# Two experts with an early part of 256 slots, and a denser routing of the last chunk but one

## The chip, the cores and the metric

The kernel runs as one program on one core of a Trainium2 chip. The metric is the device time of an execution in microseconds (us): the median of three runs.

## The reference, cut to what matters

Three layers follow one another. The first is an attention (2 batches, 8 heads, 768 positions, head size 64) in which a query sees only the keys of its own hash bucket. The second is a dense layer of 512 to 2048 to 512. The third, which the change is about, sends each of 1536 tokens to two of eight experts:

```python
noisy_logits = x @ w_gate + np.log1p(np.exp(x @ w_noise)) * noise
top2 = np.argpartition(-noisy_logits, 2, axis=1)[:, :2]
top2_l = np.take_along_axis(noisy_logits, top2, axis=1)
top2_w = np.exp(top2_l - top2_l.max(-1, keepdims=True))
top2_w /= top2_w.sum(-1, keepdims=True) + 1e-09
for e in range(8):
    for k in range(2):
        mask = top2[:, k] == e
        h = np.maximum(x[mask] @ w1[e], 0.0)          # 512 -> 1024
        out[mask] += top2_w[mask, k, None] * (h @ w2[e])   # 1024 -> 512
```

## The kernel before, in words

**Chunks.** Tokens go through attention and the dense layer in six chunks of 256 (ci 0 to 5). The order of the work is a loop over steps g: the attention has NU = 96 steps, and the loop runs 20 steps beyond. In each step a chunk of the dense layer has one of its sixteen pieces (i): eight of `h` (L460, 24 matmuls of 256 columns) and eight of `px` (L471, 12 matmuls of 512 columns), so a step of the tail is about 2.6 us of TensorE. Chunk 5 has the steps 99 to 114.

**Order.** Functions are put on lists for a step: `start` (ahead of the step's work), `soon` (after its activations), `at` (at its end). From step 100 on, the instructions of every engine, SyncE's DMA queue among them, stand in the order in which these lists emit them (`tc.manual_schedule`). Within one list the plain functions go first to last, and generators (the routing) then take turns.

**Routing.** `route(ci)` (L572) computes the gate with sixteen small matmuls into `pz`, and then some forty tiny VectorE operations with ScalarE exponentials between them; `yield 1` marks where the chain goes from one engine to the other (a hop). Its end are slot numbers `si` (L679) and four indirect DMAs of GpSimd (the scatters, L685) that write each token's row of values and metadata into `slots` in DRAM. Each expert has 400 slots (CAP). Chunk 4's routing begins in step 103 and takes a hop a step; its last part is emitted in step 110. Chunk 5's routing is spread over the first steps of the experts, eight small operations a step from step x = 2.

**Experts.** In the second loop, over x, each expert's slots are read by a transposing DMA into `xg` (`e_load`, L749, with the metadata `mt` behind it on SyncE's queue), `e_meta` (L768) makes weights and token numbers of the metadata in small VectorE operations, `l1` (L799) and `l1_out` (ScalarE L809, VectorE L810) make the hidden layer through three PSUM buffers `ph`, and `l2` (L821; its last, half-filled tile L825) and `l2_out` (ScalarE L835, then an adding scatter of GpSimd L838) the output. Weights are loaded in eight blocks of 512 KB an expert (`w12_load`, L724, SyncE's queue, four buffers `w`), and each block is split into two fp16 halves by ScalarE (L742) and VectorE (L743) in `w12_split`. Expert 0's blocks 4 to 7 are loaded in steps 107 to 110 and its splits are in steps 107 to 114. The buffers of expert 1's weights are those of the dense layer's `wo`.

**The early part.** Of the first EA = 1 experts, the first 256 slots are a part of their own. After chunk 4, `reserve` raises the count of such an expert to 256 at least, so that chunk 5's tokens go behind these slots, and this part can run while chunk 5 is still being routed. The order of parts is (0,0), (0,1), (1,0), (2,0), ...; a name (e,p) is expert e, part p.

Of the kernel before, what the change touches and what calls it, by code (L numbers as in the profile page):

```python
# [52 lines left out]
SW2 = 2.0 ** 6  # L53


PARAM = dict(GM=16, HE=lambda nm, b: 'D', OE=lambda nm, b: 'D', SC=lambda nm, b: 'D', WB=0, XO=lambda b: 'D', NG=16, WS=lambda i: 'P', TS=lambda g: True, XL=lambda g: 'D', GW=2, E0=7, T0=12, T1=16, EL=8, WX=3, PV={(1,2,3):4}, PVD=5, ST={}, VA={}, RA={}, O0=48, OS=2, IS=2, FU=16, VF=2, EC=lambda g: 'AA', QX=8, QS=3, EA=1, S1=(8,8,8,9,9,9,11,13), QE=8, XG=2, XB=2, PC=2, OH=3, BK=3, R0=18, R1=0, LK=8, WL=1, NW=3, LE=lambda nc: nc.scalar, I0=24, LQ=8, LV=0, W=[(g, 1) for g in range(-6, 30)], KA={(0,0,0):-8,(0,0,1):-6,(0,1,0):-4,(0,1,1):-2}, QA={(0,0,0):-7,(0,0,1):-3}, HI=lambda g: 'P', LO=lambda g: False)
PARAM.update(KA={(0, 0, 0): -15, (0, 0, 1): -6, (0, 1, 0): -5, (0, 1, 1): -4, (0, 2, 0): -1, (0, 2, 1): 1, (0, 3, 0): 4, (0, 3, 1): 5, (1, 0, 0): 37, (1, 0, 1): 39, (1, 1, 0): 44, (1, 1, 1): 46, (1, 2, 0): 42, (1, 2, 1): 51, (1, 3, 0): 47, (1, 3, 1): 51}, QA={(0, 0, 0): -15, (0, 0, 1): -3, (0, 0, 2): 1, (0, 0, 3): 3, (0, 1, 0): 8, (0, 1, 1): 9, (0, 1, 2): 17, (0, 1, 3): 21, (0, 2, 0): 24, (0, 2, 1): 28, (0, 2, 2): 30, (0, 2, 3): 33, (1, 0, 0): 37, (1, 0, 1): 41, (1, 0, 2): 47, (1, 0, 3): 52, (1, 1, 0): 57, (1, 1, 1): 56, (1, 1, 2): 60, (1, 1, 3): 69, (1, 2, 0): 72, (1, 2, 1): 69, (1, 2, 2): 80, (1, 2, 3): 84}, VA={(0, 0, 0): -1, (0, 0, 1): -3, (0, 1, 0): -1, (0, 1, 1): -1, (0, 2, 0): 0, (0, 2, 1): 0, (0, 3, 0): -1, (0, 3, 1): -2, (1, 0, 0): -1, (1, 0, 1): -1, (1, 1, 0): 2, (1, 1, 1): -4, (1, 2, 0): -3, (1, 2, 1): -3, (1, 3, 0): 2, (1, 3, 1): -2}, PV={(0, 0, 0): 4, (0, 0, 1): 5, (0, 0, 2): 6, (0, 0, 3): 5, (0, 1, 0): 6, (0, 1, 1): 4, (0, 1, 2): 4, (0, 1, 3): 5, (0, 2, 0): 5, (0, 2, 1): 5, (0, 2, 2): 5, (0, 2, 3): 6, (1, 0, 0): 4, (1, 0, 1): 5, (1, 0, 2): 4, (1, 0, 3): 5, (1, 1, 0): 5, (1, 1, 1): 5, (1, 1, 2): 5, (1, 1, 3): 6, (1, 2, 0): 6, (1, 2, 1): 4, (1, 2, 2): 4, (1, 2, 3): 4}, RA={0: 18, 1: 18, 2: 19, 3: 24, 4: 18}, W=[(g,1) for g in [-6, -4, -3, -1, 0, 0, 1, 1, 2, 4, 4, 7, 8, 8, 9, 10, 11, 12, 13, 14, 15, 16, 16, 17, 18, 20, 20, 22, 22, 23, 23, 24]], EC=lambda g:'AA', LE=lambda nc:nc.sync, HI=lambda g:'AAAA'[g%4], LO=lambda g:[0, 0, 0, 1, 0, 0, 0, 1][g%8]==1, S1=[8, 8, 8, 8, 8, 11, 13, 22], ST={0: 4, 1: 4, 2: 5, 3: 4, 4: 5, 5: 3}, NG=28, WS=lambda i:'PAAA'[i%4], HE=lambda nm,b:'DPDD'[2*(nm=='k')+b], OE=lambda nm,b:'DTDD'[2*(nm=='k')+b], SC=lambda nm,b:'DADD'[2*(nm=='k')+b], R1=2, I0=26, IS=1, O0=56, OS=1, GM=100, BK=3, OH=3, QX=8, QS=2, QE=7, VF=0, T0=12, T1=17, EL=10, WX=5, WL=2, PC=2, GW=2, E0=8, WB=2)


@with_exitstack  # L60
def fused(ctx: ExitStack, tc: tile.TileContext, q, k, v, proj, w_in, w_out, w_gate, w_noise, noise,
          w1, w2, out, dbg=None):
    nc = tc.nc
# [784 lines left out]
    def at(g, f, *a):  # L848
        todo.setdefault(g, []).append((f, a))

    def start(g, f, *a):
# [4 lines left out]

    def piece(gen):
        for x in gen:
            if x:
                return  # L860
            yield
# [98 lines left out]
    for g in range(g_lo, G1 + 1):  # L960
# [7 lines left out]
        prev = steps.get(g - 1, [])  # L968
# [183 lines left out]
```

## Time and profile before

| | us |
|---|---|
| median of 3 runs (lowest, highest) | 825.37 (823.86, 825.7) |
| the profiled execution | 823.72 |
| its span | 822.0 |
| TensorE busy | 715.9 (87%) |
| VectorE busy | 533.9 (65%) |
| ScalarE busy | 445.0 (54%) |
| GpSimd busy | 267.9 (33%) |

The span runs from the first to the last instruction; what lies around it is 1.72 us. Busy time is a mean over stages with different limits. The change is about the hand-over from the dense layer to the experts, at 500 to 610 us of the span, so that stretch is read by itself: for each engine its instructions in order of time, with the idle time before one and what ended it.

### The profile page before, as it was taken

How to read it: one execution, taken by the hardware profiler on the slowest of the kernel's cores; microseconds unless marked ns; L12 is line 12 of the kernel's file. 1: busy time of each engine (PE TensorE's matmuls, PEld its weight loads, DVE VectorE, ACT ScalarE, POOL GpSimd, SP SyncE). 2: the span in 40 equal slices, each digit the busy share in tenths (PEclk: the TensorE clock that was granted, in tenths of full speed). 3: DMA queues.
4: the chain of work that ended last, by engine and by line, in shares of the span. 5: the costliest groups of instructions: out<-in, count | busy, mean ns of one | idle time of the engine just before them, and what ended most of it. 6: DMA issues, size and time to landing. Idle time of an engine off the chain costs nothing.

```text
span 822.0 us, 14816 instructions
## 1 busy us (share of the span) xinstructions
PE 715.9 (87%) x5398; PEld 446.0 (54%) x5399; DVE 533.9 (65%) x1330; ACT 445.0 (54%) x859; POOL 267.9 (33%) x303
## 2 busy tenths in 40 slices
PE   1676478988988888898999999879999999999995
PEld 1343345646754665466568576547554655556553
DVE  8998799997896789569869526454633525345210
ACT  3778767766765686467567425234533534334220
POOL 6444646560444055314212132241021120311212
PEclk9878789999999999999999999999999999999998
DMA  8999689999999999995797542856875858677213
GB/s 218 224 251 212 180 187 184 255 277 218 175 171 195 154 200 192 225 159 106 119 176 123 102 156 88 221 146 180 250 158 173 199 111 232 135 194 176 28 19 47
DMA packets 268126, 140.04 MB, mean 170 GB/s; under 512 B 224720, under 2 KB 243856, under 8 KB 268048
## 3 DMA queue, kind: packets, MB, share of 16 engines
q1 hardware_dynamic: 261520, 125.37, 68.1%
q0 software_dynamic: 6528, 13.68, 9.3%
q8 instruction: 43, 0.70, 0.4%
q14 instruction: 35, 0.29, 0.1%
HBM read 61.48 MB, written 23.79 MB: 104 GB/s over the span
## 4 chain that ended last, share of the span: by engine, by line
PE 42%; DVE 5%; DMA 3%; POOL 2%; issue 1%; ACT 1%; POOLq 0%; ACTq 0%; DVEq 0%
PE ph L799 15%; PE py L821 13%; PE px L471 6%; PE h L460 3%; PE py L825 2%; DVE er L323 1%; DMA xg<-slots 1%; PE pv L368 1%; POOL slots L685 1%; DMA slots<-xr,si 1%; DMA et<-er 1%; PE s L254 1%; ACT er L314 1%; DVE e L266 1%; DVE th L490 1%
## 5 line engine op out<-in xcount | busy, mean ns | idle before, releaser
L460 PE MATMUL h<-xt,wi 128*128 128x256 f16 x1152 | 140.2, 277 | 6.2 <-DVE mx L279 3.2
L799 PE MATMUL ph<-xg,ew 128*128 128x400 f16 (+2 forms) x864 | 135.4, 320 | 8.9 <-DMA xg<-slots 8.4
L743 DVE SCALAR_TENSOR_TENSOR ew<-w,ew 128x1024 f16<-128x1024 f32 x64 | 77.9, 1226 | 88.2 <-ACT ew L742 88.0
L471 PE MATMUL px<-wo,gt 128*128 128x512 f16 x576 | 132.6, 382 | 0.5 <-DVE th L490 0.4
L460 PEld LDWEIGHTS <-wi 128*128 128x128 f16 x1152 | 112.5, 99 | 28.2 <-issue 9.1
L821 PE MATMUL py<-ew,ht 128*128 128x512 f16 x576 | 125.8, 379 | 0.0
L838 POOL DMA_INDIRECT out_dram<-yo,ti x32 | 51.2, 1600 | 216.7 <-ACT yo L835 216.7
L254 PE MATMUL s<-kt,qt 128*128 128x512 f16 (+1 forms) x384 | 88.2, 353 | 33.3 <-DVE mx L266 28.5
L799 PEld LDWEIGHTS <-ew 128*128 128x128 f16 x864 | 82.6, 100 | 59.8 <-issue 6.8
L275 ACT ACTIVATE e<-e,mx 128x768 f32<-128x768 f32 x96 | 89.4, 931 | 27.9 <-DVE mx L266 21.5
L505 POOL TENSOR_TENSOR gt<-th,gt 128x512 f16<-128x512 f32 x48 | 60.1, 1252 | 122.0 <-ACT gt L504 121.6
L266 DVE CUSTOM_DVE_ANT_0 e<-s,zero 128x768 f32<-128x768 f32 x96 | 90.6, 948 | 4.4 <-PE s L254 1.5
L821 PEld LDWEIGHTS <-ht 128*128 128x128 f16 x576 | 56.3, 98 | 67.0
L471 PEld LDWEIGHTS <-gt 128*128 128x128 f16 x576 | 55.3, 98 | 64.1 <-issue 3.2
L323 DVE SCALAR_TENSOR_TENSOR er<-e,mx,er 128x768 f16<-128x768 f32 x68 | 73.1, 1080 | 25.9 <-ACT er L314 25.3
L314 ACT ACTIVATE er<-e,mx 128x768 f16<-128x768 f32 x68 | 63.0, 930 | 37.8 <-DMA et<-er 21.6
L835 ACT ACTIVATE yo<-py,wv 128x512 f32<-128x512 f32 (+1 forms) x32 | 20.3, 633 | 102.4 <-PE py L821 54.6
L809 ACT ACTIVATE ht<-ph 128x400 f16<-128x400 f32 (+2 forms) x72 | 33.5, 466 | 73.0 <-PE ph L799 72.9
L254 PEld LDWEIGHTS <-qt 128*128 128x128 f16 x384 | 37.0, 103 | 62.7 <-issue 38.5
L810 DVE SCALAR_TENSOR_TENSOR ht<-ph,ht 128x400 f16<-128x400 f32 (+2 forms) x72 | 37.6, 524 | 49.5 <-ACT ht L809 49.5
L742 ACT ACTIVATE ew<-w 128x1024 f16<-128x1024 f32 x64 | 66.3, 1047 | 2.6 <-DMA w<-in_moe_w_dram 2.6
L368 PE MATMUL pv<-et,vt 128*64 128x256 f16 x720 | 51.2, 284 | 7.5 <-DMA et<-er 7.5
(195 smaller groups left out, 945.8 us busy)
## 6 DMA issues: line engine op xcount, KB each, us to landing
w<-in_moe_w_dram SPq DMA_DIRECT2D x64, 512.0 KB, 4.6
wraw<-in_moe_w_in_dram SPq DMA_DIRECT2D x16, 512.0 KB, 4.6
wraw<-in_moe_w_out_dram SPq DMA_DIRECT2D x16, 512.0 KB, 4.3
slots<-blank SPq DMA_DIRECT2D x6, 1032.0 KB, 6.8
v<-in_v_dram SPq DMA_DIRECT2D x24, 192.0 KB, 4.1
out_dram<-zeros SPq DMA_DIRECT2D x13, 256.0 KB, 3.4
k<-in_k_dram SPq DMA_DIRECT2D x16, 192.0 KB, 3.6
q<-in_q_dram SPq DMA_DIRECT2D x24, 128.0 KB, 3.1
```

The costliest lines, as they stand in the source:

```text
L254: nc.tensor.matmul(ps[:, n0 * 128:n1 * 128], qt[:, s, h, t, :], kt[:, s, h, n0:n1, :].rearrange("p c t -> p (c t)"), start=(s == 0), stop= ...
L266: nc.vector.tensor_tensor_reduce(e32, st[g]["ps"][:, :S], zero.to_broadcast([128, S]), -0.125, TOP, op0=OP.add, op1=OP.min, accum_out=mx[: ...
L275: nc.scalar.activation(e32, e32, AF.Exp, scale=-1.0, bias=st[g]["mx"][:, 1:2], accum_out=sms[b, cc, hp][:, 2 * h + t:2 * h + t + 1] if g < ...
L314: nc.scalar.activation(er[:, 0], st[g]["e"], AF.Copy, scale=r)
L323: nc.vector.scalar_tensor_tensor(er[:, 1], d["e"], d["mx"][:, 3:4], er[:, 0], op0=OP.mult, op1=OP.subtract)
L460: nc.tensor.matmul(ph[:, a, :], wi[ws][:, d, f0:f0 + 128], xt[:, d, xs, :], start=(d == 0 and ws == 0 and xs == 0), stop=(d == HP - 1 and ...
L471: nc.tensor.matmul(px, gts[ci, f // 2][:, gs, f % 2, t * 128:t * 128 + 128], wo[ws][:, f, :], start=(f == 0 and gs == 0 and ws == 0), stop ...
L505: nc.gpsimd.tensor_tensor(gt[:, 1], th, gt[:, 0], op=OP.subtract)
L742: nc.scalar.activation(hi, x, AF.Copy, scale=SW1 if j == 0 else SW2)
L743: nc.vector.scalar_tensor_tensor(lo, x, SW1 if j == 0 else SW2, hi, op0=OP.mult, op1=OP.subtract)
L799: nc.tensor.matmul(ph[:, :c1 - c0], w[:, ws, d * FE + f * 128:d * FE + f * 128 + 128], xg[e, p][:, xs * HP + d, :], start=(d == 0 and ws = ...
L821: nc.tensor.matmul(py, ht[:, f, hs, t * 128:t * 128 + 128], w[:, ws, f * DM:(f + 1) * DM], start=(i == 0), stop=(i == n - 1))
```

## The change

Five things are changed (EA and S1 stand in the table PARAM; chunks 0 to 3 keep the seven lines of the routing). EA is 2: experts 0 and 1 have an early part, and the order of parts becomes (0,0), (1,0), (0,1), (1,1), (2,0), .... Chunk 4's routing takes two hops in steps 104 and 105, so its last part is emitted in step 107 and not 110, `reserve` in 108, and the loads of the early parts, now two, in step 110 and not 113. Expert 1's splits (S1) are spread from x = 2 on, four of them before x = 8. The metadata of the early parts are computed at x = 3 and x = 6. Expert 2's splits, and the loads and metadata of the second parts, are placed by the new order.

```diff
-EA=1
+EA=2
-S1=[8, 8, 8, 8, 8, 11, 13, 22]
+S1=[2, 3, 4, 6, 9, 10, 12, 14]
...
+    def one(gen):
+        next(gen)
...
             start(r0, next, gen)
             at(r0, piece, gen)
-            for i in range(1, 4):
-                soon(r0 + i, next, gen)
-                at(r0 + i, piece, gen)
-            at(r0 + 4, piece, gen)
-            start(r0 + 5 + r1, next, gen)
-            at(r0 + 5 + r1, piece, gen)
-            if ci == B * NCH - 2:
-                at(r0 + 6 + r1, done, gen)
-                at(r0 + 6 + r1, reserve)
+            if ci < B * NCH - 2:
...
+            else:
+                start(r0 + 1, next, gen)
+                soon(r0 + 1, whole, piece(gen))
+                at(r0 + 1, one, gen)
+                start(r0 + 2, whole, piece(gen))
+                soon(r0 + 2, next, gen)
+                at(r0 + 2, piece, gen)
+                at(r0 + 3, piece, gen)
+                start(r0 + 4, next, gen)
+                at(r0 + 4, piece, gen)
+                at(r0 + 5, done, gen)
+                at(r0 + 5, reserve)
                 for e in range(EA):
-                    at(r0 + PARAM["E0"] + r1, e_load, e, 0)
-                    at(r0 + PARAM["E0"] + 2 + r1, e_meta, e, 0)
+                    at(r0 + 7, e_load, e, 0)
...
+    for e in range(EA):
+        at(3 + 3 * e, e_meta, e, 0)
     for e in range(1, E):
         prev = gs[gs.index((e, 0)) - 1]
-        if e >= EA + 1:
-            b0, b1 = begin[prev], begin[e, 0]
+        if e >= EA:
+            b0, b1 = begin[prev if e > EA else (0, 1)], begin[e, 0]
         for i in range(8):
-            x = b0 + (b1 - b0) * i // 8 if e >= EA + 1 else PARAM["S1"][i]
+            if e < EA:
+                x = PARAM["S1"][i]
+            elif e > EA:
+                x = b0 + (b1 - b0) * i // 8
+            else:
+                x = b0 + 9 + 2 * i if i < 4 else begin[1, 1] + 2 * (i - 1)
             at(x - PARAM['WX'], w12_load, e, i)
             at(x, w12_split, e, i)
     for e, p in gs[EA:]:
         if p == 1:
-            b0 = PARAM["QE"] + e
-            at(b0, done, gen)
+            b0 = PARAM["QE"] if e == 0 else begin[e, 0] + 8
+            if e == 0:
+                at(b0, done, gen)
             at(b0, e_load, e, p)
-            at(b0 + 1, e_meta, e, p)
+            at(begin[e, p] - 3, e_meta, e, p)
```

## Rows read from the trace of the kernel before

**Rows 1.** The page's head: the span.

```profile
span 822.0 us, 14816 instructions
```

**Rows 2.** PE's timeline: start, duration, line, tiles, shape, count, idle before.

```profile
490.55 10.64 PE L460 MATMUL h<-xt,wi 128*128 128x256 f16 x96
...
525.76 4.35 PE L799 MATMUL ph<-xg,ew 128*128 128x256 f16 x24 [3.77 <-DMA xg<-slots]
529.91 0.31 PE L578 MATMUL pz<-wg,xrt 128*128 128x32 f16 x4
...
553.92 6.30 PE L799 MATMUL ph<-xg,ew 128*128 128x144 f16 x72 [4.61 <-DMA xg<-slots]
```

**Rows 3.** The chain that ended last, expert 1 alone: start, duration, work.

```profile
572.49 16.26 PE ph L799 x96
588.75 15.54 PE py L821 x72
604.29 2.74 PE py L825 x48
```

**Rows 4.** VectorE's timeline over the two routings.

```profile
504.95 1.33 DVE L743 SCALAR_TENSOR_TENSOR ew<-w,ew 128x1024 f16<-128x1024 f32 x1 [1.64 <-ACT ew L742]
...
511.37 0.16 DVE L655 TENSOR_SCALAR d<-d 128x2 f32<-128x2 f32 x1
...
512.93 0.17 DVE L679 CAST si<-sf 128x4 int32<-128x4 f32 x1
...
522.65 0.69 DVE L494 SCALAR_TENSOR_TENSOR xr<-px,xr 128x512 f16<-128x512 f32 x1 [3.72 <-ACT xr L485]
...
530.80 0.19 DVE L586 TENSOR_TENSOR z<-zc 128x32 f32<-128x32 f32 x1 [2.37 <-ACT zc L583]
...
537.30 0.42 DVE L810 SCALAR_TENSOR_TENSOR ht<-ph,ht 128x256 f16<-128x256 f32 x1
...
538.35 0.17 DVE L679 CAST si<-sf 128x4 int32<-128x4 f32 x1
...
540.35 4.63 DVE L743 SCALAR_TENSOR_TENSOR ew<-w,ew 128x1024 f16<-128x1024 f32 x4 [0.52 <-ACT ew L742]
```

**Rows 5.** GpSimd's timeline: the first two scatters of chunk 5.

```profile
539.29 0.96 POOL L685 DMA_INDIRECT slots<-xr,si  x1 [19.44 <-DVE mt L764]
...
540.55 1.85 POOL L685 DMA_INDIRECT slots<-xr,si  x1 [0.21 <-issue]
```

**Rows 6.** SyncE's queue: start and time of issue.

```profile
506.32 5.53 SPq L731 DMA_DIRECT2D w<-in_moe_w_dram  x4
...
521.61 2.03 SPq L756 DMA_TRANSPOSE xg<-slots  x1
...
524.36 1.24 SPq L570 DMA_TRANSPOSE xrt<-xr  x1
...
549.10 1.30 SPq L756 DMA_TRANSPOSE xg<-slots  x1
...
552.07 0.38 SPq L731 DMA_DIRECT2D w<-in_moe_w_dram  x1
```

**Rows 7.** ScalarE's timeline: the last splits of expert 0, then chunk 5's xr.

```profile
514.33 2.94 ACT L742 ACTIVATE ew<-w 128x1024 f16<-128x1024 f32 x3
522.02 0.60 ACT L485 ACTIVATE xr<-px 128x512 f16<-128x512 f32 x1 [4.75 <-PE px L471]
```

**Rows 8.** The page's part 5: VectorE's half of a split, count, busy, mean ns.

```profile
L743 DVE SCALAR_TENSOR_TENSOR ew<-w,ew 128x1024 f16<-128x1024 f32 x64 | 77.9, 1226 | 88.2 <-ACT ew L742 88.0
```

**Rows 9.** DMA issues of 500 to 560 us: count, size, us to landing.

```profile
w<-in_moe_w_dram SPq DMA_DIRECT2D x12, 512.0 KB, 4.1
```

**Rows 10.** Tile w over the run: the 64 weight blocks, issue to landing.

```profile
DMA to landing us min/median/max: 3.5/4.6/7.4
```

**Rows 11.** Tile xrt over the run: the chunks' transposed rows, issue to landing.

```profile
DMA to landing us min/median/max: 3.0/3.6/6.6
```

**Rows 12.** PE's busy time and granted clock (last but two) around the restart.

```profile
527.00:528.00 1.00, 1.00 (x7) 0.50 0.67 147
```

More of the change, by code (lines that the diff above doesn't have):

```diff
@@ L53 @@
 SW2 = 2.0 ** 6
-PARAM = dict(GM=16, HE=lambda nm, b: 'D', OE=lambda nm, b: 'D', SC=lambda nm, b: 'D', WB=0, XO=lambda b: 'D', NG=16, WS=lambda i: 'P', TS=lambda g: True, XL=lambda g: 'D', GW=2, E0=7, T0=12, T1=16, EL=8, WX=3, PV={(1,2,3):4}, PVD=5, ST={}, VA={}, RA={}, O0=48, OS=2, IS=2, FU=16, VF=2, EC=lambda g: 'AA', QX=8, QS=3, EA=1, S1=(8,8,8,9,9,9,11,13), QE=8, XG=2, XB=2, PC=2, OH=3, BK=3, R0=18, R1=0, LK=8, WL=1, NW=3, LE=lambda nc: nc.scalar, I0=24, LQ=8, LV=0, W=[(g, 1) for g in range(-6, 30)], KA={(0,0,0):-8,(0,0,1):-6,(0,1,0):-4,(0,1,1):-2}, QA={(0,0,0):-7,(0,0,1):-3}, HI=lambda g: 'P', LO=lambda g: False)
@@ new lines @@
+PARAM = dict(GM=16, HE=lambda nm, b: 'D', OE=lambda nm, b: 'D', SC=lambda nm, b: 'D', WB=0, XO=lambda b: 'D', NG=16, WS=lambda i: 'P', TS=lambda g: True, XL=lambda g: 'D', GW=2, E0=7, T0=12, T1=16, EL=8, WX=3, PV={(1,2,3):4}, PVD=5, ST={}, VA={}, RA={}, O0=48, OS=2, IS=2, FU=16, VF=2, EC=lambda g: 'AA', QX=8, QS=3, EA=2, S1=(8,8,8,9,9,9,11,13), QE=8, XG=2, XB=2, PC=2, OH=3, BK=3, R0=18, R1=0, LK=8, WL=1, NW=3, LE=lambda nc: nc.scalar, I0=24, LQ=8, LV=0, W=[(g, 1) for g in range(-6, 30)], KA={(0,0,0):-8,(0,0,1):-6,(0,1,0):-4,(0,1,1):-2}, QA={(0,0,0):-7,(0,0,1):-3}, HI=lambda g: 'P', LO=lambda g: False)
@@ new lines @@
+PARAM.update(KA={(0, 0, 0): -15, (0, 0, 1): -6, (0, 1, 0): -5, (0, 1, 1): -4, (0, 2, 0): -1, (0, 2, 1): 1, (0, 3, 0): 4, (0, 3, 1): 5, (1, 0, 0): 37, (1, 0, 1): 39, (1, 1, 0): 44, (1, 1, 1): 46, (1, 2, 0): 42, (1, 2, 1): 51, (1, 3, 0): 47, (1, 3, 1): 51}, QA={(0, 0, 0): -15, (0, 0, 1): -3, (0, 0, 2): 1, (0, 0, 3): 3, (0, 1, 0): 8, (0, 1, 1): 9, (0, 1, 2): 17, (0, 1, 3): 21, (0, 2, 0): 24, (0, 2, 1): 28, (0, 2, 2): 30, (0, 2, 3): 33, (1, 0, 0): 37, (1, 0, 1): 41, (1, 0, 2): 47, (1, 0, 3): 52, (1, 1, 0): 57, (1, 1, 1): 56, (1, 1, 2): 60, (1, 1, 3): 69, (1, 2, 0): 72, (1, 2, 1): 69, (1, 2, 2): 80, (1, 2, 3): 84}, VA={(0, 0, 0): -1, (0, 0, 1): -3, (0, 1, 0): -1, (0, 1, 1): -1, (0, 2, 0): 0, (0, 2, 1): 0, (0, 3, 0): -1, (0, 3, 1): -2, (1, 0, 0): -1, (1, 0, 1): -1, (1, 1, 0): 2, (1, 1, 1): -4, (1, 2, 0): -3, (1, 2, 1): -3, (1, 3, 0): 2, (1, 3, 1): -2}, PV={(0, 0, 0): 4, (0, 0, 1): 5, (0, 0, 2): 6, (0, 0, 3): 5, (0, 1, 0): 6, (0, 1, 1): 4, (0, 1, 2): 4, (0, 1, 3): 5, (0, 2, 0): 5, (0, 2, 1): 5, (0, 2, 2): 5, (0, 2, 3): 6, (1, 0, 0): 4, (1, 0, 1): 5, (1, 0, 2): 4, (1, 0, 3): 5, (1, 1, 0): 5, (1, 1, 1): 5, (1, 1, 2): 5, (1, 1, 3): 6, (1, 2, 0): 6, (1, 2, 1): 4, (1, 2, 2): 4, (1, 2, 3): 4}, RA={0: 18, 1: 18, 2: 19, 3: 24, 4: 18}, W=[(g,1) for g in [-6, -4, -3, -1, 0, 0, 1, 1, 2, 4, 4, 7, 8, 8, 9, 10, 11, 12, 13, 14, 15, 16, 16, 17, 18, 20, 20, 22, 22, 23, 23, 24]], EC=lambda g:'AA', LE=lambda nc:nc.sync, HI=lambda g:'AAAA'[g%4], LO=lambda g:[0, 0, 0, 1, 0, 0, 0, 1][g%8]==1, S1=[2, 3, 4, 6, 9, 10, 12, 14], ST={0: 4, 1: 4, 2: 5, 3: 4, 4: 5, 5: 3}, NG=28, WS=lambda i:'PAAA'[i%4], HE=lambda nm,b:'DPDD'[2*(nm=='k')+b], OE=lambda nm,b:'DTDD'[2*(nm=='k')+b], SC=lambda nm,b:'DADD'[2*(nm=='k')+b], R1=2, I0=26, IS=1, O0=56, OS=1, GM=100, BK=3, OH=3, QX=8, QS=2, QE=7, VF=0, T0=12, T1=17, EL=10, WX=5, WL=2, PC=2, GW=2, E0=8, WB=2)
@@ L938, in fused @@
             at(r0, piece, gen)
-            for i in range(1, 4):
-                soon(r0 + i, next, gen)
-                at(r0 + i, piece, gen)
-            at(r0 + 4, piece, gen)
-            start(r0 + 5 + r1, next, gen)
-            at(r0 + 5 + r1, piece, gen)
-            if ci == B * NCH - 2:
-                at(r0 + 6 + r1, done, gen)
-                at(r0 + 6 + r1, reserve)
+            if ci < B * NCH - 2:
+                for i in range(1, 4):
+                    soon(r0 + i, next, gen)
+                    at(r0 + i, piece, gen)
+                at(r0 + 4, piece, gen)
+                start(r0 + 5 + r1, next, gen)
+                at(r0 + 5 + r1, piece, gen)
+            else:
[7 more added lines that the diff above has]
+                start(r0 + 4, next, gen)
+                at(r0 + 4, piece, gen)
+                at(r0 + 5, done, gen)
+                at(r0 + 5, reserve)
                 for e in range(EA):
-                    at(r0 + PARAM["E0"] + r1, e_load, e, 0)
-                    at(r0 + PARAM["E0"] + 2 + r1, e_meta, e, 0)
+                    at(r0 + 7, e_load, e, 0)
     for i in range(4):
@@ L1009, in fused @@
     at(20, r_counts)
+    for e in range(EA):
+        at(3 + 3 * e, e_meta, e, 0)
     for e in range(1, E):
         prev = gs[gs.index((e, 0)) - 1]
-        if e >= EA + 1:
-            b0, b1 = begin[prev], begin[e, 0]
-        else:
-            pass
+        if e >= EA:
+            b0, b1 = begin[prev if e > EA else (0, 1)], begin[e, 0]
         for i in range(8):
-            x = b0 + (b1 - b0) * i // 8 if e >= EA + 1 else PARAM["S1"][i]
+            if e < EA:
[4 more added lines that the diff above has]
+                x = b0 + 9 + 2 * i if i < 4 else begin[1, 1] + 2 * (i - 1)
             at(x - PARAM['WX'], w12_load, e, i)
```

1 line of the change is left out of this document (removed).

## The prediction, made before the changed kernel was run

> **What bounds the kernel now.** I read the page's head first (span 822.0 us; the profiled execution took 823.72, so 1.72 lie around the span [rows 1]), then TensorE's timeline over the hand-over [rows 2]: it stands still twice, 3.77 us until `xg` of (0,0) lands and 4.61 until `xg` of (0,1) does, and each pause drags a slow restart behind it: the first 24 matmuls of 256 columns after the first take 4.35 us, where 96 of that shape take 10.64 in the stretch before (0.109 each, 2.6 for 24), and 72 of 144 columns take 6.30 after the second, where 4.5 would do (below). That is 1.7 and 1.8 on top of the pauses. Outside this stretch the chain of waits is TensorE's own matmuls, expert after expert [rows 3]: 16.26 for the 96 of L799 (0.169 each), 5.18 for each of three tiles of L821, 2.74 for L825. So the change can win or lose only between about 500 and 607 us (604.29 + 2.74 = 607.03, where expert 1 and the first L1 block of expert 2 are through). Two pauses and two slow restarts are some 12 us: the most to be had.
>
> **Extra matmuls.** Expert 1 split into 256 and 144 slots adds 96 matmuls. A line through 256 columns at 0.109 and 400 at 0.169 gives 0.062 for 144, and 0.109 + 0.062 = 0.171 against 0.169: 0.2 us in all. I count zero; the eight extra evacuations by ScalarE and VectorE lie beside blocks of 0.74 us, and are shorter.
>
> **Chunk 4's routing.** It is written three steps earlier, 7.9 us, but does not finish that much earlier. Its last part then stands in step 107 behind the first weight split of expert 0, whose VectorE half ran from 504.95 to 506.28 [rows 4], since a plain function goes before a generator. The part itself took from 511.37 (L655) to 513.10 (`si`), 1.73. So `si` comes at about 508.0 and not 513.10: 5.1 earlier. The small matmuls `pp` and `pt` of steps 107 and 108 may hold TensorE up for under 1 us each, for VectorE is only just ready; that delays the end of `px`, and is covered by the longer wait below. From `si`, the four scatters and their landing took 513.10 to 521.61 = 8.5 for chunk 4, and 538.52 to 549.10 = 10.6 for chunk 5, whose second scatter ran 1.85 beside VectorE's splits where its first took 0.96 [rows 5]. I take 8.5, the stretch of the same scatters with the same splits beside them: landed at 516.5 (bound 518.6).
>
> A rule bears on this. The Trainium skill, "SBUF — State Buffer", section "SBUF: two separate sides", says that a VectorE instruction with two SBUF inputs and a GpSimd one that reads SBUF lock each other out of a shared port for a whole instruction. The split's VectorE half has two SBUF inputs. By the rule in full, all four scatters would be held as the 1.85 one was, some 3 us more than I take. Chunk 4's 8.5 in all, with splits beside it, do not show that for each, so I leave it to the dear rival.
>
> **SyncE's queue.** This is where I expect the loss. Step 110 emits both `e_load`s, and behind them, because it was put on the list later, the load of expert 0's last weight block, w(0,7). In the kernel before that load went out as the last of four issues from 506.32 to 511.85, ahead of everything [rows 6]. SyncE's queue holds what is behind a waiting issue: the block issued at 552.07 had its buffer since the split halves that VectorE ran from 540.35 to 544.98 [rows 4], but went out only behind `xg` of (0,1), which waited for the scatters until 549.10. So w(0,7) now waits for the scatters (516.5) and for two loads of `xg` and `mt`, each 524.36 - 521.61 = 2.75: it goes out at 522.0, ten us later. Queued behind it in turn: ScalarE's split of w(0,7) in step 114 stands before chunk 5's second `xr` (step 115), and in the kernel before `xr` began at 522.02, right when `px` ended, the splits long done, each 1.0 of ScalarE [rows 7] and 1.23 of VectorE [rows 8]. Now: landing 4.1 us after issue (the stretch's median [rows 9], bounds 3.5 and 7.4 by the whole run's blocks [rows 10]) gives 526.1; the two halves, 2.2, give 528.3; `xr` on VectorE 0.69 [rows 4] gives 529.0; the transposition `xrt` 3.0 to 6.6, I take 3.2, near the shortest, as nothing else then moves [rows 11]: 532.2. The routing's gate matmuls (`pz`) of chunk 5, at x = 2, stood at 529.91 before [rows 2] and now wait until 532.2. The first pause goes, because `xg` of (0,0) lands at about 520.6 (4.1 after 516.5); but TensorE gets only two L1 blocks (2.6 us) done before it meets `pz` at 524.6, and stands still for about 7.5 us. The second wait takes the first one's place and is longer.
>
> **VectorE between `pz` and the ninth L1 block.** The order in the kernel is now: (0,0)'s eight L1 blocks, then one of (1,0), which needs expert 1's first four splits. These are emitted among the routing's pieces at x = 2, 3, 4 and 6. In the kernel before, VectorE went from `z` at 530.80 to the end of the sixth `l1_out` at 537.72 [rows 4], 6.9 us, with the splits from 540.35 on. To these come four VectorE halves at 1.23 = 4.9; two `e_meta` of six small operations each, of the size of L655's 0.16 but overlapped: together 1.3 (bounds 0.8 and 2.0); and a wait for the first block, which is queued behind `xrt`: issue 529.0 + 1.24, landing + 4.1, ScalarE + 1.0 = 535.4, where VectorE would be free at about 534.3, 1.1. Sum 14.2; if the halves fall into the pauses that VectorE has anyway, 1.5 less. `z` comes 0.7 after `pz` can start: 532.9. So the ninth L1 block starts at 547.1 and ends 12 × 0.109 = 1.3 later, 548.4. TensorE stands still in between, for it needs only 8 us of matmuls there: at `ph` buffers, and for some 4 us at `pp` of x = 6. The restart after a pause is slow: behind the 3.77 us of idle time the granted clock fell to 0.50, that is 1.2 GHz [rows 12], and the 1.7 above are its price. The one after `pz` lies beside VectorE's work and costs nothing; the one after `pp` falls on the last two or three blocks: I take 1.3 of 1.7. The ninth block ends at 549.7.
>
> **The rest.** From there it is TensorE's work without a wait: six tiles of L821 at 5.18 and two L825 at 2.74 = 36.6; L1 seven blocks of 256 at 1.31, sixteen of 144 at 0.74 and one of 400 at 2.03 = 23.1; together 59.7. Chunk 5's rows are in `slots` by 559, long before (0,1) is due at about 579, so the second pause is gone with its slow restart; its price is what stands above. Expert 1's last block w(1,7) goes out only behind `xg` of (0,1), at about 560, and is wanted at 564: 0 to 1.6, I take 0.2. Expert 2's first splits stand in seven L1 steps of 0.74 us, with 1.0 of ScalarE each: 0 to 1, I take 0.2. So 549.7 + 59.7 + 0.4 = 609.8 against 607.03: 2.8 us later. From there on nothing is changed.
>
> **The sum.** 823.72 + 2.8 = 826.5 by the profiled execution. That one lies 1.65 under the median of the runs, 825.37; on the median the forecast is 828.2. About 0.2%, 1.65 us, can be told from no change.
>
> **Rivals.**
> *The load is not held* (the other side). If w(0,7) is landed and split before `px` ends, `xr` is ready at 522.0 as before, `xrt` leaves at 523.3 and lands by 526.4; all that follows comes 5.8 earlier: 2.8 - 5.8 = -3.0, 822.4. It decides at 522.0 - 2.2 (both halves) - 4.1 = 515.7: if the load goes out by then. For it: the transfers themselves have room. Against it: the issue at 552.07. A page speaks for it as far as it goes: the Trainium skill, "DMA: Bandwidth & Descriptors", section "Issuing engines are not separate DMA queues", puts what a shared issuing engine costs at its time to issue, usually small. It does not tell of an issue that waits.
> *Both waits are hidden.* TensorE runs from 522.0 through nine blocks (11.8) and `pz` (0.5) and then the 59.7: 594.0, 13.0 earlier, 812.4. For it: the two early parts are 41 us of TensorE's work, longer than chunk 5's whole routing and landing (523.3 to 553.9 before). Against it stands that VectorE alone has 14 us of work before the ninth block.
> *Dear.* Scatters held by the splits as above (3 us), w(1,7) late (1.6 at most): 2.8 + 4.6 = 7.4, 832.8. For it the 10.6 of chunk 5's scatters; against it chunk 4's own 8.5.
>
> **How the numbers follow.** Forecast 0.50, load not held 0.20, both hidden 0.08, dear 0.22. The forecast's bounds are -2 (the overlap in VectorE, no slow restart) and +3 (landing), 826.2 to 831.2. Range 820.5 to 834.5: it leaves out both-hidden, a little of the second case and the worst of the dear one, some 0.17. Faster: 0.08, most of the second case's 0.20, 0.03 of the forecast's low end, together 0.25. Within 0.2%: 0.06 of the second case and 0.14 of the forecast, 0.20. Slower: 0.55.
>
> **What the profile after would show.** On SyncE's queue, two `xg` loads at about 516.5 and the w load only behind them at about 522; ScalarE idle before the last split of expert 0 until about 526, then `xr`; no pause of TensorE at 522, one of about 7 us at 524.6 that `pz` ends near 532; another of some 4 us that `pp` ends; `si` of chunk 5 near 548 and not 538.5; no pause before (0,1). I am wrong in the step on the queue if the w load leaves before the `xg` loads, in the step on VectorE if the ninth block follows the eighth at once, and in the step on chunk 4 if `xg` leaves at 513 or at 521.

## The result, and the profile after

The changed kernel takes 833.24 us (median of 4 runs, 831.98 to 834.52) against 824.62 for the kernel before (4 runs, 823.68 to 825.7): ratio 1.0096 [1.008, 1.0113], 8.6 us slower. A second measurement of the same two kernels gave 1.0082 [1.0054, 1.0111]. The forecast was 828.2, 2.8 us slower. The side was right and 833.24 lies within the range, but the loss is about three times the size that was forecast.

Two executions can't be compared by their spans alone. Up to chunk 4's gate matmuls, the first `pz` at L578, nothing is changed, and yet they began at 490.15 us in the profile before, at 492.69 in the one after, and anywhere from 487.33 to 492.20 in the others. So times below are counted from that matmul to the end of expert 1 and the first L1 block of expert 2: the **stretch**. It is 607.03 - 490.15 = 116.9 us before [rows 3], 122.6 after. Behind its end the spans of both kernels have the same 215.0 us left, in two profiles of each. The fence is TensorE's timeline of the kernel after (start, duration, line, tiles, shape, count, idle before and its releaser), which answers to [rows 2, 3].

```profile
492.69 0.26 PE L578 MATMUL pz<-wg,xrt 128*128 128x32 f16 x4
...
509.71 15.70 PE L471 MATMUL px<-wo,gt 128*128 128x512 f16 x72
532.99 5.05 PE L799 MATMUL ph<-xg,ew 128*128 128x256 f16 x24 [7.58 <-DVE xr L494]
537.88 0.25 PE L578 MATMUL pz<-wg,xrt 128*128 128x32 f16 x4
...
548.28 0.19 PE L650 MATMUL pp<-mk,before 128*128 128x16 f16 x1 [3.61 <-DVE mk L633]
548.47 0.17 PE L651 MATMUL pp<-cum,one 128*128 128x16 f16 x1
548.50 5.46 PE L799 MATMUL ph<-xg,ew 128*128 128x256 f16 x36
553.79 10.52 PE L821 MATMUL py<-ew,ht 128*128 128x512 f16 x48
564.15 9.33 PE L799 MATMUL ph<-xg,ew 128*128 128x256 f16 x84
...
601.54 3.23 PE L799 MATMUL ph<-xg,ew 128*128 128x144 f16 x48 [0.64 <-DVE ht L810]
605.25 2.19 PE L799 MATMUL ph<-xg,ew 128*128 128x400 f16 x12 [0.49 <-ACT ht L809]
...
612.55 2.81 PE L825 MATMUL py<-ew,ht 128*64 128x256 f16 x48
615.29 2.88 PE L799 MATMUL ph<-xg,ew 128*128 128x400 f16 x16
```

Both pauses on `xg` of [rows 2] are gone. In their place stand 7.58 us ahead of the first L1 block, ended by `xr`, and 3.61 ahead of `pp`, with a slow restart behind each (24 matmuls in 5.05, 36 in 5.46, where 12 such matmuls take 1.3 at the full clock). What holds `xr` is read from the queue. The next fence is SyncE's queue after (start and time of issue); it answers to [rows 6].

```profile
509.09 4.86 SPq L731 DMA_DIRECT2D w<-in_moe_w_dram  x3
520.56 1.89 SPq L756 DMA_TRANSPOSE xg<-slots  x1
...
523.11 2.15 SPq L756 DMA_TRANSPOSE xg<-slots  x1
...
525.98 0.41 SPq L731 DMA_DIRECT2D w<-in_moe_w_dram  x1
```

Three of expert 0's last four weight blocks go out; the fourth, w(0,7), stands behind both `xg` loads and leaves at 525.98. ScalarE's timeline after, the answer to [rows 7], shows who waits for it: the split of that block, with chunk 5's second `xr` behind it.

```profile
530.02 1.06 ACT L742 ACTIVATE ew<-w 128x1024 f16<-128x1024 f32 x1 [9.91 <-DMA w<-in_moe_w_dram]
530.98 0.58 ACT L485 ACTIVATE xr<-px 128x512 f16<-128x512 f32 x1
```

Step by step, in us from chunk 4's first gate matmul, for the kernel after in the profile shown and in a second one. Forecast times are those of the prediction less 490.15.

| | forecast | after | after, second profile |
|---|---|---|---|
| `si` of chunk 4 written | 17.9 | 18.0 | 19.0 |
| first `xg` leaves (scatters landed) | 26.4 | 27.9 | 29.2 |
| w(0,7) leaves | 31.9 | 33.3 | 34.8 |
| chunk 5's second `xr` done | 38.9 | 40.2 | 42.0 |
| `pz` of chunk 5 starts | 42.1 | 45.2 | 47.1 |
| ninth L1 block ended | 59.6 | 61.1 | 63.4 |
| end of the stretch (before: 116.9) | 119.7 | 122.6 | 124.9 |

Both profiles are slower in the stretch than forecast, by 2.95 and 5.3 us. The second is nearer to what the medians, 833.24 and 832.41, ask for. As an estimate: with the gate matmul at 489.9, the middle of all thirteen profiles, and 1.7 us around the span, a stretch of 124.9 makes 489.9 + 124.9 + 215.0 + 1.7 = 831.5, and one of 122.6 makes 829.2. Where the time lies is the question of the experiments.

### The profile page after: what moved, and what is told of

Same layout as the page of the kernel before. It is cut to its first block, busy times and chain, and to the rows that moved or that the text cites. A ratio compares the mean times of both kernels' runs of the same rounds, so it can differ in the third digit from the quotient of the medians.

```text
span 830.3 us, 15034 instructions
## 1 busy us (share of the span) xinstructions
PE 719.7 (87%) x5494; PEld 453.5 (55%) x5495; DVE 536.6 (65%) x1344; ACT 446.4 (54%) x867; POOL 265.7 (32%) x303
## 4 chain that ended last, share of the span: by engine, by line
PE 37%; DVE 6%; DMA 3%; ACT 3%; issue 2%; POOL 1%; SPq 1%; POOLq 0%; ACTq 0%; DVEq 0%
PE ph L799 15%; PE py L821 14%; PE px L471 3%; DMA et<-er 2%; PE py L825 2%; PE h L460 2%; DVE er L323 1%; ACT ew L742 1%; DVE ew L743 1%; ACT er L314 1%; DVE th L490 1%; DVE e L266 1%; DMA slots<-xr,si 1%; PE pv L368 1%; POOL slots L685 0%
## 5 line engine op out<-in xcount | busy, mean ns | idle before, releaser
L460 PE MATMUL h<-xt,wi 128*128 128x256 f16 x1152 | 142.9, 280 | 7.4 <-DVE th L490 4.3
L799 PEld LDWEIGHTS <-ew 128*128 128x128 f16 x960 | 88.3, 100 | 56.4 <-issue 11.6
L809 ACT ACTIVATE ht<-ph 128x400 f16<-128x400 f32 (+2 forms) x80 | 34.8, 437 | 63.4 <-PE ph L799 62.7
```

What stands on the lines that cost most here:

```text
L460: nc.tensor.matmul(ph[:, a, :], wi[ws][:, d, f0:f0 + 128], xt[:, d, xs, :], start=(d == 0 and ws == 0 and xs == 0), stop=(d == HP - 1 and ...
L799: nc.tensor.matmul(ph[:, :c1 - c0], w[:, ws, d * FE + f * 128:d * FE + f * 128 + 128], xg[e, p][:, xs * HP + d, :], start=(d == 0 and ws = ...
```

## The experiments

**The kernel before, again.** No edit; it shows how far two measurements of one kernel lie apart.

> The kernel before, unchanged, as a second look at it. In its first profile the gate matmuls of chunk 4 stood at 490.15 us, in that of the changed kernel at 492.69, though up to there both issue the same instructions. If that 2.5 us is a property of the changed program, this profile shows 490.2 again; if executions differ that much in the attention, it lies anywhere between 489 and 494. Time ratio to the kernel before: 1.000 within 0.002.

Ratio 0.9999 [0.9973, 1.0024], stretch 117.7. The runs of the kernel before on that chip went from 821.33 to 830.61, so one time alone can't tell a difference of a few us, and the stretch in the profile is read beside each ratio.

**The kernel after, again.** No edit.

> The changed kernel, unchanged, in more rounds and with a second profile. The attention ahead of the change differs by several us from one execution to the next (chunk 4's gate matmuls stood at 487.3 to 492.7 in six profiles of one and the same instructions), so the stretch is measured from these matmuls to the end of expert 1 and expert 2's first block: 116.9 and 117.7 us in two profiles before, 122.7 in that of the change. If 5 to 6 us is what the change costs, the ratio is 1.006 to 1.008, and the rest of the first 1.0096 was the attention's spread; if the change also costs time ahead of that stretch, 1.009 to 1.011.

1.0082 [1.0054, 1.0111], stretch 124.9, with the same pauses: 8.35 us before the first L1 block, ended by `xr`, and 3.62 before `pp`.

**The load not held.** Both `e_load`s one step later, so that w(0,7) stands ahead of them on SyncE's queue.

```diff
-                    at(r0 + 7, e_load, e, 0)
+                    at(r0 + 8, e_load, e, 0)
```

> The changed kernel, with both loads of xg one step later, so that the load of expert 0's last weight block stands ahead of them on SyncE's queue. Queue theory: that block is split by 519, xr of chunk 5 is ready right behind px (526), TensorE's first expert block starts at about 526.7 and not 533.0, the gate matmuls of chunk 5 come near 530 and not 537.9; all after it moves by 7 to 8 us: span 822 to 824, ratio to the kernel before 0.998 to 1.003. VectorE theory (the four splits among chunk 5's routing are the bound, whenever it starts): the ninth block ends at 552 or later as in the changed kernel (553.9), under 2 us gained, ratio 1.007 to 1.010.

1.0027 [0.9996, 1.0058], stretch 119.2. So taking the hold away gives 1.0082 or 1.0096 less 1.0027, 4.5 to 5.7 us (3.4 and 5.7 by the stretches; 7 to 8 were expected); the prediction priced it at 5.8. It is a net price, since the scatters, which now have the fourth block beside them, land 2.4 to 2.7 us later after `si`. But without the hold the kernel should have been 3.0 us faster than before by the prediction's sum, and it is 2.2 slower (-0.3 to 4.8). Something else costs about 5 us. TensorE's timeline of this run has a pause on `xg` again, and SyncE's queue below it says when `xg` could leave.

```profile
487.33 0.26 PE L578 MATMUL pz<-wg,xrt 128*128 128x32 f16 x4
...
522.10 4.45 PE L799 MATMUL ph<-xg,ew 128*128 128x256 f16 x24 [2.07 <-DMA xg<-slots]
527.17 0.26 PE L578 MATMUL pz<-wg,xrt 128*128 128x32 f16 x4 [0.62 <-DMA xrt<-xr]
```

```profile
503.71 6.00 SPq L731 DMA_DIRECT2D w<-in_moe_w_dram  x4
517.89 1.92 SPq L756 DMA_TRANSPOSE xg<-slots  x1
```

The scatters' own timeline on GpSimd ends early, with the last of the four:

```profile
510.59 0.96 POOL L685 DMA_INDIRECT slots<-xr,si  x1 [0.22 <-issue]
```

So `xg` left 517.89 - 511.55 = 6.3 us after the last scatter; in the kernel before it was 521.61 - (517.80 + 1.97) = 1.8.

**VectorE's work taken away, the load still held.** Expert 1's splits go behind (0,0), no ninth block ahead of (0,0)'s second layer.

```diff
-S1=[2, 3, 4, 6, 9, 10, 12, 14]
+S1=[8, 8, 8, 8, 11, 13, 15, 16]
...
-        if n and (p == 0 or n > EA):
+        if n > 1 and (p == 0 or n > EA):
```

> The changed kernel, with no block of expert 1 ahead of (0,0)'s second layer, and expert 1's first four splits behind chunk 5's routing (x = 8). The load of expert 0's last block stays behind the xg loads. VectorE theory: from the gate matmuls on, eight blocks take 8 to 9 us and not 16; 5 to 7 us gained, ratio 1.001 to 1.004. Queue theory alone: TensorE still stands still until 533, and what VectorE no longer does early it does late; under 2 us gained, ratio 1.007 to 1.010. If both waits are paid one after the other, both this and the run before gain, and their gains add up in the next.

1.01 [1.0045, 1.0155], stretch 124.4: nothing gained. The congestion did go (`pp` waits 0.72 and not 3.61), and (0,0)'s second layer begins 57.2 after the gate matmul, against 61.1 in the kernel after. It is given back 20 us later, as TensorE's timeline shows:

```profile
546.67 10.52 PE L821 MATMUL py<-ew,ht 128*128 128x512 f16 x48
...
567.64 4.45 PE L799 MATMUL ph<-xg,ew 128*128 128x256 f16 x24 [2.59 <-DVE ht L810]
```

On SyncE's queue the last three weight blocks of expert 1 leave at 559.35, behind `xg` of (0,1), which waited for chunk 5's scatters until 555.87; ScalarE's split waits 3.40 for them. It is the first held load again, one expert on, and made by my edit.

**Both edits.** The load ahead and VectorE's work taken away.

```diff
-                    at(r0 + 7, e_load, e, 0)
+                    at(r0 + 8, e_load, e, 0)
...
-S1=[2, 3, 4, 6, 9, 10, 12, 14]
+S1=[8, 8, 8, 8, 11, 13, 15, 16]
...
-        if n and (p == 0 or n > EA):
+        if n > 1 and (p == 0 or n > EA):
```

> Both edits at once. If the two waits lie one behind the other, the gains add up: first expert block at about 526.7, no wait until expert 2, span 813 to 816, ratio to the kernel before 0.987 to 0.991, which beats it. If one wait only hides the other, no more than the better of the two alone.

1.0002 [0.9969, 1.0035], stretch 117.3: a miss by 8 to 11 us. Two of the reasons are seen above, in this run's own numbers: `xg` leaves 521.46 - 514.68 = 6.8 after the last scatter, and the late blocks of expert 1 cost a wait of 2.49. That put the scatters' landing in front.

**The routing's two hops alone.** The kernel before with nothing but the denser routing of chunk 4: EA = 1, one load, still in step 113.

```diff
-            for i in range(1, 4):
-                soon(r0 + i, next, gen)
-                at(r0 + i, piece, gen)
...
+                start(r0 + 1, next, gen)
+                soon(r0 + 1, whole, piece(gen))
+                at(r0 + 1, one, gen)
+                start(r0 + 2, whole, piece(gen))
```

> The kernel before, with chunk 4's routing in two hops a step and nothing else: one early part, xg's load still in step 113. Collision theory: the slot numbers come 5 us earlier, but the scatters then run into the loads of expert 0's blocks 4 to 7 and land little earlier (30 to 32 us behind chunk 4's gate matmuls, 31.5 before); the stretch stays at 116 to 118, ratio 0.998 to 1.001. Rival, that the routing's lead is kept: the scatters land near 26.5, the first pause of 3.8 us and its slow restart go, stretch 111 to 113, ratio 0.993 to 0.995.

1.0018 [0.9996, 1.0040]: no gain, as the theory of the collision had it. The stretch is 124.4 and not the 116 to 118 expected. But the profiled execution, 831.95, is the slowest of ten with a median of 827.01, and its pause on `xg` of (0,1) is 9.39 us, where it is 4.61 and 4.95 in the kernel before; so its times are those of the longest execution. In it the change's second part, which stands by itself here, makes the slots **later**. The last scatter ended 516.81 - 490.88 = 25.9 after the gate matmul, where it was 29.6 before, and `xg` left at 34.0 where it was 31.5. GpSimd's timeline, then SyncE's queue, then the DMA view of 503 to 526 us (size, count, median us to landing):

```profile
510.17 1.72 POOL L685 DMA_INDIRECT slots<-xr,si  x1 [2.98 <-DVE si L679]
...
515.70 1.11 POOL L685 DMA_INDIRECT slots<-xr,si  x1 [0.21 <-issue]
```

```profile
508.27 5.42 SPq L731 DMA_DIRECT2D w<-in_moe_w_dram  x4
...
524.89 1.84 SPq L756 DMA_TRANSPOSE xg<-slots  x1
```

```profile
slots<-xr,si POOLq DMA_INDIRECT x4, 9.4
```

In the kernel before, the four weight blocks left from 506.32 to 511.85 [rows 6], ahead of the first scatter, as its GpSimd timeline shows, and the scatters' median was 4.6.

```profile
513.38 0.99 POOL L685 DMA_INDIRECT slots<-xr,si  x1 [8.15 <-DVE si L679]
...
517.80 1.97 POOL L685 DMA_INDIRECT slots<-xr,si  x1 [0.22 <-issue]
```

The denser routing brings the scatters forward, into the loads: 9.4. In this run chunk 5's first `xrt`, issued at 514.53, moves among them too.

**The loads out of the scatters' way.** The edit of the load not held, and all eight blocks of expert 0 in step 99, into eight buffers.

```diff
-        x = m2.tile([128, 1024], F32, name="w32", bufs=4)
+        x = m2.tile([128, 1024], F32, name="w32", bufs=8)
...
-                    at(r0 + 7, e_load, e, 0)
-    for i in range(4):
+                    at(r0 + 8, e_load, e, 0)
+    for i in range(8):
         at(NU + 3, w12_load, 0, i)
...
-        if i < 4:
-            at(NU + 11 + i, w12_load, 0, i + 4)
```

> The run with the load first, and eight buffers w instead of four, so that all eight blocks of expert 0 are loaded in step 99 and no weights move while chunk 4 is scattered. Collision theory: the scatters land within 8.5 us of the slot numbers (12.8 in the run with the load first), both xg loads leave before px ends, TensorE's pause there is about 1.3 us (until VectorE's xr frees the bank), chunk 5's gate matmuls come 36 to 37 us behind chunk 4's (40 in the run with the load first, 39.8 before), stretch 115 to 117, ratio 0.995 to 0.999. Rival: the scatters are as slow without the loads, stretch 119 as in the run with the load first, ratio 1.002.

0.9975 [0.9952, 0.9998], 2.1 us faster than before (0.2 to 4.0), where the prediction's rival without the held load said 3.0. The stretch, 116.8, is hardly shorter than before (116.9 and 117.7). Against the run that only moved the load it is 0.0052, 4.3 us, by the ratios and 2.4 by the stretches; the scatters' landing is 6.3 - 1.9 = 4.4 shorter, of which `si`, 1.0 later here, takes back one. GpSimd's timeline, SyncE's queue and the DMA view of this run:

```profile
509.18 1.71 POOL L685 DMA_INDIRECT slots<-xr,si  x1 [2.98 <-DVE si L679]
511.19 1.38 POOL L685 DMA_INDIRECT slots<-xr,si  x1 [0.21 <-issue]
...
514.15 0.96 POOL L685 DMA_INDIRECT slots<-xr,si  x1 [0.22 <-issue]
```

```profile
517.00 1.89 SPq L756 DMA_TRANSPOSE xg<-slots  x1
```

```profile
slots<-xr,si POOLq DMA_INDIRECT x4, 2.8
```

Over all thirteen profiles, the time from the end of the last scatter to the issue of the first `xg`:

| weight blocks leaving beside the scatters | us |
|---|---|
| none (this run, the three below with eight buffers, the two of before) | 1.8 to 2.0 |
| three (the two profiles of after, late splits, own banks below) | 3.6, 4.0, 4.9, 5.0 |
| four (load not held, both edits, two hops alone with `xrt` among them) | 6.3, 6.8, 8.1 |

**The first block's buffers.** The kernel after has TensorE's first L1 block wait for `xr`, not for `xg` (landed long before). A rival theory was that this order costs the missing time: `ph` gets the PSUM banks that `px` held, and the whole of them must have been read. Here `h` and `px` have banks of their own, and `py` two buffers for three.

```diff
+    psh = ctx.enter_context(tc.tile_pool(name="psh", bufs=2, space=bass.MemoryType.PSUM))
...
-            px = psum.tile([128, 2, CQ], F32, name="px", tag="h")
+            px = psh.tile([128, 2, CQ], F32, name="px", tag="h")
...
-        py = psum2.tile([128, DM], F32, name="py", bufs=3)
+        py = psum2.tile([128, DM], F32, name="py", bufs=2)
```

> The changed kernel, with the tiles h and px in a PSUM pool of their own that stays open, so that the experts' ph takes other banks (py has two buffers for three). It tests the step of the prediction that failed: TensorE's first expert block waited for VectorE's xr. If that was a bank shared with px, two blocks now run at the end of px or when xg lands, ahead of chunk 5's gate matmuls, which then wait for xrt at 43 to 44 us behind chunk 4's gate matmuls (45.2 and 47.1 in the two profiles of the changed kernel); 1.5 to 3 us gained, ratio 1.004 to 1.007. If the first block waits for something else on that chain, it still starts only when xr ends, and the ratio stays at 1.008.

1.0077 [1.0051, 1.0102], stretch 125.4, against 1.0082 and 124.9 without the edit: nothing. TensorE's timeline of this run (its lines are one higher) shows that the cause was named rightly and its price wrongly.

```profile
525.17 2.78 PE L800 MATMUL ph<-xg,ew 128*128 128x256 f16 x24 [0.57 <-DMA xg<-slots]
531.87 0.27 PE L579 MATMUL pz<-wg,xrt 128*128 128x32 f16 x4 [3.92 <-DMA xrt<-xr]
...
536.88 0.29 PE L579 MATMUL pz<-wg,xrt 128*128 128x32 f16 x4 [4.65 <-DMA xrt<-xr]
...
548.25 6.74 PE L800 MATMUL ph<-xg,ew 128*128 128x256 f16 x36
```

The first two blocks run at once, at the full clock, and the second half of `pz` starts 3.1 after `xr` (533.76), not 5.15 as in the kernel after (538.08 - 532.93). But TensorE then waits twice for `xrt`, and from there to the end of the ninth block it takes 554.82 - 536.88 = 17.9, not 15.7. From `xr` to the end of the ninth block it is 21.1 here and 20.9 and 21.4 in the two profiles of the kernel after.

**VectorE's work, with the loads out of the way.** The early loads, expert 1's splits behind (0,0) (S1 = 8, 8, 8, 8, 9, 9, 12, 14), no ninth block ahead, and expert 1's blocks loaded early enough not to stand behind `xg` of (0,1):

```diff
-            at(x - PARAM['WX'], w12_load, e, i)
+            at(i - 3 if e < EA else x - PARAM['WX'], w12_load, e, i)
```

> The run with early loads (ratio 0.9975, stretch 116.9), with expert 1's splits behind chunk 5's routing, no block of expert 1 ahead of (0,0)'s second layer, and expert 1's blocks loaded ahead of the second part's xg. Expert 2's splits stay where the change put them. It prices the splits among the routing by themselves: VectorE theory 14 us of work for 8 us of matmuls, that is 6 to 7 us gained, stretch 110 to 111, ratio 0.989 to 0.991, and the remaining 1.3 us to the run of all edits are expert 2's. Rival: that the gain of the run of all edits came from expert 2's splits or the loads' order; under 3 us, ratio above 0.993.

0.9904 [0.9875, 0.9932], 815.59 us; stretch 110.2, 6.6 us less than with the loads out of the way alone (5.9 by the ratios), as expected. The three edits go together here, and the run doesn't divide the gain among them. TensorE's timeline has no pause over 1.5 us left:

```profile
523.37 2.78 PE L799 MATMUL ph<-xg,ew 128*128 128x256 f16 x24 [1.41 <-DVE xr L494]
...
532.80 0.18 PE L650 MATMUL pp<-mk,before 128*128 128x16 f16 x1 [0.72 <-DVE mk L633]
...
584.69 3.23 PE L799 MATMUL ph<-xg,ew 128*128 128x144 f16 x48 [0.63 <-DVE ht L810]
```

**And expert 2's splits.** The same, with expert 2's first four splits ahead of the short blocks of (1,1) and not among them.

```diff
-                x = b0 + 9 + 2 * i if i < 4 else begin[1, 1] + 2 * (i - 1)
+                x = b0 + (8, 9, 9, 10)[i] if i < 4 else begin[1, 1] + 2 * (i - 1)
```

> The run before, with expert 1's first six splits behind chunk 5's routing, no block of expert 1 ahead of (0,0)'s second layer, expert 1's blocks loaded ahead of the second part's xg, and expert 2's first splits three steps earlier. If the waits that the runs have shown (queue, collision, VectorE among the routing, late blocks of expert 1, crowded splits of expert 2) are all there are: stretch 105 to 109, ratio 0.986 to 0.991, faster than the kernel before. If a further wait takes their place, stretch above 113 and ratio above 0.994.

0.987 [0.9837, 0.9903], 815.83 us (814.18 to 816.74); stretch 108.7, 1.5 less than without this edit, by one profile of each. The 0.63 above is gone, and the seven short blocks with the first of expert 2 take 592.00 - 584.71 = 7.3 us, where the run above takes 590.43 - 581.63 = 8.8, as does the kernel after. The ratios alone, 0.987 and 0.9904, don't tell these two apart.

```profile
584.71 7.46 PE L799 MATMUL ph<-xg,ew 128*128 128x144 f16 x96
592.00 5.34 PE L821 MATMUL py<-ew,ht 128*128 128x512 f16 x24
```

**And own banks.** That kernel with the banks of the edit further above.

```diff
+    psh = ctx.enter_context(tc.tile_pool(name="psh", bufs=2, space=bass.MemoryType.PSUM))
...
-            px = psum.tile([128, 2, CQ], F32, name="px", tag="h")
+            px = psh.tile([128, 2, CQ], F32, name="px", tag="h")
```

> The run of all edits (ratio 0.987, stretch 108.7), with the same banks of their own for h and px. Its last pause at the hand-over is 1.41 us until xr frees the bank. If the two blocks then run in it, 1 to 1.5 us more: stretch 107 to 108, ratio 0.984 to 0.987. If xrt, which lands no earlier, takes its place (the gate matmuls at x = 2), no gain: 0.986 to 0.988.

0.9881 [0.9858, 0.9904], 815.06 us (812.09 to 816.41), stretch 107.7. The first block now starts when `px` ends, and `pz` takes over the wait (1.64 for `xrt`): again no difference that can be told. Both versions beat the kernel before by some 10 us, and the kernel after by more.

## Why the forecast had the side right and the size wrong

**The queue: right.** w(0,7) left behind both `xg` loads, 5.4 and 5.6 us after the first of them went (forecast 5.5); ScalarE stood 9.91 us for it, and from its issue to `xr` 7.0 and 7.2 us went by (forecast 7.0). The run with the load ahead gives 4.5 to 5.7 us for it, forecast 5.8, though net of its own later landing.

**The scatters: the step that failed.** "I take 8.5, the stretch of the same scatters with the same splits beside them: landed at 516.5 (bound 518.6)." The splits were the same; the loads were not. Three blocks left from 509.09 to 513.95, among the scatters, whose first and last on GpSimd's timeline after are

```profile
510.99 1.72 POOL L685 DMA_INDIRECT slots<-xr,si  x1 [2.98 <-DVE si L679]
...
515.97 0.96 POOL L685 DMA_INDIRECT slots<-xr,si  x1 [0.22 <-issue]
```

and from `si` to the landing it took 9.85 us, 10.2 in the second profile and 11.2 in the run with own banks. The 8.5 was measured where the loads had gone ahead, and the change itself moved the scatters into them. Two hops alone show it without any held load, if in the longest of its executions, and with the loads gone it is 8.1 in all four profiles. It was 1.4 to 2.7 us of the missing time, and with the fourth block beside them, as the rival of the load not held has it, 4.

The rule that I weighed there did not decide. In the kernel after, the first two scatters take 1.72 and 1.38 us and the last two 0.96, and the run without loads beside has 1.71, 1.38 and 0.96 with the same splits; all four run 5.94 us from first start to last end, 6.39 before. The Trainium skill, "SBUF — State Buffer", section "SBUF: two separate sides", would have the first two held by VectorE's port, and that agrees, but it costs nothing more than before.

What did decide is the traffic on the DMA engines. The Trainium skill, "DMA: Bandwidth & Descriptors", section "Queues, rings and completion order", says that the increment which reports a DMA done lands only after all earlier writes of the same DMA engine, whatever their queue; by that, scatters that have landed could be reported late behind weight blocks. The traces, which record every packet, show another thing: the scatters' own packets move late. In the kernel after, the last weight packet ends at 518.52 and the last packet of the scatters at 519.93, and `xg` leaves at 520.56. The DMA view from 518.55 to 520.56 us (queue, packets, MB, share; q0 are the scatters, 320 packets and 1.06 MB in all) has a third of them starting only there, and no weights:

```profile
q0 software_dynamic: 102, 0.30, 37.7%
q1 hardware_dynamic: 1, 0.00, 0.0%
```

In all thirteen traces `xg` leaves 0.3 to 0.8 us after the scatters' last packet, and no weight packet ends after that one. The first scatter's first packet starts 4.1 us behind its instruction in the kernel after (510.99 to 515.11) and 2.3 in the run without the loads (509.18 to 511.47).

**The step at TensorE: wrong in its order, right in its price.** "TensorE gets only two L1 blocks (2.6 us) done before it meets `pz` at 524.6": it got none, since the first block itself waited for `xr`. The two blocks then ran behind `xr`, at the granted clock of 0.50, which is 1.2 GHz, to which it had fallen while TensorE stood still (the windows after, with the clock last but two; 538 to 540 is back at 1.00):

```profile
528.00:530.00 2.00, 0.00 (x0) 0.00 (x0) 0.00 (x0) 0.00 (x0) 0.00 (x0) 0.50 1.06 315
...
534.00:536.00 2.00, 2.00 (x11) 1.40 (x10) 0.00 (x0) 0.26 (x1) 0.00 (x0) 0.50 0.86 160
```

That made `pz` 1.8 us late against 3.2 after `xr`. The way from there to the ninth block's end was 1.6 shorter than forecast, with the 3.61 before `pp` (forecast some 4). From `xr` to the ninth block's end: forecast 20.7, measured 20.9 and 21.4, and 21.1 where the blocks did run ahead. VectorE's work sets that stretch, as the prediction said, whatever TensorE does first.

**The rest: too small.** "Expert 2's first splits ... 0 to 1, I take 0.2." From the ninth block to the end of the stretch, 61.5 us in both profiles, forecast 60.1: 1.4 more. The waits of 0.64 and 0.49 in the short blocks are their mark, and moving them ahead gave 1.5 back. The late w(1,7), priced at up to 1.6, cost nothing: 84 matmuls of expert 1 run from 564.15 without a wait, and the second layer, which needs that block, follows at 573.32.

**Chunk 4's `si`: 1.0 short, most of the time.** Forecast 17.9 after the gate matmul, measured 18.0 and 19.0; over the eleven profiles with the denser routing it is 18.0 in three and 19.0 in eight. The prediction called a wait at `pp` covered. That wait, 0.5 us in the eight and none in the three, doesn't make `si` late. Both come from one place further up the routing, where a small VectorE operation and a GpSimd subtraction begin within 0.01 us of each other. VectorE's and GpSimd's timelines of the kernel after, first profile and second:

```profile
501.00 0.17 DVE L615 TENSOR_TENSOR rw<-z,rw 128x16 f32<-128x16 f32 x1
501.00 1.20 POOL L505 TENSOR_TENSOR gt<-th,gt 128x512 f16<-128x512 f32 x1 [1.58 <-ACT gt L504]
...
496.58 1.18 DVE L615 TENSOR_TENSOR rw<-z,rw 128x16 f32<-128x16 f32 x1
496.57 1.16 POOL L505 TENSOR_TENSOR gt<-th,gt 128x512 f16<-128x512 f32 x1 [1.58 <-ACT gt L504]
```

In the eight profiles the VectorE operation takes 1.18 us beside GpSimd's 1.16, in the three it takes 0.17, and all that hangs on it, `mk` for `pp` and then `si`, comes 1.0 later. The prediction had no term for it.

**The sum.** Over the forecast's 2.77 us, in the profile shown: `si` 0.17, scatters 1.35, the queue and the split -0.13, `xr` to ninth block 0.16, rest 1.40: 2.95, which makes the 5.7 of the stretch (122.6 - 116.9). In the second profile: 1.17, 1.67, 0.33, 0.70, 1.40: 5.27, which makes 8.0. So no single term carries the miss: the scatters are the largest, and the rest and, in most executions, `si` come close. The medians say 6.8 to 8.6; 1 to 3 us of a single pair lie in how one execution differs from another. The rival called dear had the right time, 832.8, by the wrong cause: not VectorE holding the scatters, and no late block. As the range reached up to 834.5 for that rival, it is luck that it holds 833.24.

## What to carry to other kernels

A duration taken from the old profile holds for the old neighbours. When a step is moved, list what runs beside it at its new place, on the DMA engines too: in the run with two hops alone, scatters that were brought forward 4 us landed 2.5 us later, because the move put them among 512 KB loads. On a queue that takes its issues in order, look for the load that now stands behind a waiting one, and after mending it look for the next; two of these experiments only moved the same mistake to another expert.

## What the runs showed of the hardware that was not expected

- Four scatters were reported landed 1.8 to 2.0 us after the last one ended with no weight block leaving beside them, 3.6 to 5.0 with three and 6.3 to 8.1 with four. Their own packets moved late: the report followed the last of them by 0.3 to 0.8 us in all thirteen traces.
- A VectorE operation on 128x16 values, 0.17 us by itself, took 1.18 beside a GpSimd subtraction of 1.16. That was so in eight of eleven profiles and not in the other three, and `si` came at 19.0 and at 18.0 by that.
- The same instructions, up to chunk 4's gate, ended anywhere within 5.4 us (487.33 to 492.69) from execution to execution, 4.9 of it on one chip, which is more than most of the edits are worth.
